# Four tiles with one rest phase in the up projection of an mLSTM and GELU kernel

## The chip, the cores and the metric

The kernel runs on one core of one Trainium2 chip, as one launch. The metric is the time on the device in microseconds (us), the median of several executions.

## The reference

Two parts are joined. The first is an mLSTM cell over batch 4, 8 heads, 768 steps and a head dimension of 40. The second is a plain two-layer network over the 3072 tokens of 320 features that the first part yields.

```python
for t in range(S):
    m_new = maximum(f[t] + m, i[t])
    C = exp(f[t] + m - m_new) * C + exp(i[t] - m_new) * outer(v[t], k[t])
    n = exp(f[t] + m - m_new) * n + exp(i[t] - m_new) * k[t]
    y[t] = sigmoid(o[t]) * (C @ q[t]) / maximum(abs(n @ q[t]), 1.0)
x = y as (B*S, H*D) = (3072, 320)
h = x @ w_in                      # (3072, 2048)
g = 0.5 * h * (1 + erf(h / sqrt(2)))
out = g @ w_out                   # (3072, 320)
```

All inputs are float32 but the two weight matrices, which the kernel converts from 64-bit floats as their bits lie in memory.

## The kernel before

**Stages.** The sequence is cut into six chunks of 128 steps. A chunk of all four batches is 512 tokens (TG). For each chunk the cell part makes x (its transpose, xT, in SBUF), the up step makes g = gelu(x w_in), and the down step makes g w_out. The cell work of chunk c+1 is dealt out between the products of the down step of chunk c. The first chunk and the cell part of the second are played from the string FRONT, in which conversions of the weights, loads, cell steps and up and down steps of chunk 0 are interleaved by hand. The later chunks are played from the string DOWN. So the instruction order on each engine is the written order: the pools are under manual_schedule, and each engine works in order. Semaphores between engines are set from what each instruction reads and writes.

**Letters of FRONT.** O and L load v and o, and q and k; P fetches a piece of weights; K and J are the two halves of a conversion (conv_one: three VectorE and two ScalarE instructions, conv_two: two VectorE instructions); Z adds parts of w_in; E, N, D and Q make the gate sums and decays. m, w, g, t, s, c, v, y, x are the cell steps of chunk 0 (mask, weights, gate, turn, scores, carry, values, finish, turn_y) for a batch, in capitals those of chunk 1. A and U are up steps of chunk 0, F a row of its down step. I n asks for n products into a bank that nobody reads, at the next place that calls unread; a later I before that place replaces it. They keep TensorE from idling.

**The up step of chunks 1 to 5 (summed_up, L589).** x and w_in are cut into blocks of two halves each: w_in by features 0 to 127 and 128 to 255 (x = 0, 1) and by hidden halves (e), x by the same features and by token halves (h). For these 256 features the product of 2 x 2 blocks is done with seven products instead of eight, from sums made ahead: in_sums of w_in (in_sum), x_sums of x (sum_x). The remaining 64 features are added directly, as the rest phase: their products use 64 rows, one hidden half on the upper and one on the lower half of the array (halves, w_rest). f0 counts pairs of hidden tiles, and there are four of them. For each, c11, p6, p5, c22, c12, c21 each take a bank of PSUM (128 x 512 float32) in turn from four kinds of banks, two of each, by bank() (L596). A product (L604) is two matmuls in the code and four matmul instructions in the trace.

The seven products make the four blocks so: c11's first product is copied to g (ScalarE, L611); p6 is added to it (VectorE, L614); p5 is added to that (L617); c22 is added to p6's sum (L620). c12, c21 and the second product of c11 follow; then come the 16 rest instructions (L629). After that ScalarE takes the gelu of c11 (L634), and for c22, c12 and c21 VectorE adds the partial sums (L636) and ScalarE takes the gelu in place (L637).

**Sums of g (hidden_sums, L520).** The down step also uses seven products, from sums s1 and s2 of blocks of g and a block of differences. They are made by three VectorE instructions (L525 to L527) for two tiles each, right after the rest phase of the following pair has been issued. In chunk 1 the sums of w_out for the down step (weight_sum, L507) are made around the up step: the first before it, the second after it, the others within DOWN.

**The down step (down_steps, L661).** Its product (L674) has 16 instructions; the first two (p1) read only g as it stands, the next two (p6) read s2 and, on the other side, the second sum of w_out.

Of the kernel before, what the change touches and what calls it, by code (L numbers as in the profile page):

```python
# [9 lines left out]
F32 = mybir.dt.float32  # L10
BF16 = mybir.dt.bfloat16
U32 = mybir.dt.uint32
AF = mybir.ActivationFunctionType
OP = mybir.AluOpType

P = 128
# [6 lines left out]


FRONT = """
    O0 L0 P0 I3 g0 L2 P1 E I2 t0 N w0 L1 K P2 D w1 Q O2 s0 P3 w2 t1 O1 c0 J v0 K t2 s1 w3 L3 g1 v1 I3 O3 J y0 c1 K
    B5 y1 s2 x0 O4 t3 L4 J x1 K B4 L5 g3 s3 I7 v2 g2 c2 c3 y2 G0 v3 x2 K J A L6 y3 M1 J x3 M0 K H K O7 O5 J T0 J W0
    O6 A S0 K W1 M2 J C0 T1 U U K K Z V0 J T2 L7 A M3 W2 J G1 S1 C1 Z W3 A K K G2 S2 Y0 C2 Z J J K V1 T3 G3 K U U Y1
    S3 Z C3 J V2 K F F F J Z K J J K K J Z K J F F J V3 K X0 K F J Z F J F F F K J K Y2 K J X1 K F F F J K J F J F Z
    X2 B8 B9 Y3 X3 F"""  # L30
DOWN = """
    M0 Z M1 T0 W0 F F T1 W1 Z G3 Z F S0 Z S1 C0 M2 Z C1 G1 G0 M3 V0 Y0 Z V1 W2 Z F F T2 W3 F T3 F G2 Z Y1 S2 S3 C2
    V2 C3 Y2 V3 F F Y3 X0 F F X1 X2 F F X3 F"""
# [3 lines left out]
def kernel(  # L37
# [16 lines left out]
    nc = tc.nc  # L54

    B, H, S, D = q.shape
# [11 lines left out]
    NX = 2  # L68
# [12 lines left out]
    ps_tr = ctx.enter_context(tc.tile_pool(name="ps_tr", bufs=2, space=bass.MemoryType.PSUM))  # L81
    ps_h = ctx.enter_context(tc.tile_pool(name="ps_h", bufs=2, space=bass.MemoryType.PSUM))
    ps_mm = ctx.enter_context(tc.tile_pool(name="ps_mm", bufs=2, space=bass.MemoryType.PSUM))
# [9 lines left out]
    w_rest = const.tile([P, DFF // 2], F32, name="w_rest")  # L93
# [4 lines left out]
    xT = const.tile([P, NX + 1, TG], F32, name="xT")  # L98
# [60 lines left out]
    a = gates.tile([BH, NCH, L], F32, name="a")  # L159
# [114 lines left out]
    def conv_one(i):  # L274

        if i < len(pieces):
            n = bits[i].shape[1]
            lo, hi = bits[i][:, :, 0], bits[i][:, :, 1]
            s = sig[i] = raw.tile([P, WP], F32, name="sig", tag="sig")[:, 0:n]
            p = pow2[i] = raw.tile([P, WP], F32, name="pow", tag="pow")[:, 0:n]  # L280
            su, pu = s.bitcast(U32), p.bitcast(U32)

            nc.vector.tensor_scalar(out=pu, in0=hi, scalar1=20, scalar2=0x7FF,
                                    op0=OP.logical_shift_right, op1=OP.bitwise_and)
            nc.scalar.activation(out=p, in_=pu, func=AF.Relu, scale=-I23, bias=e_hi)
            nc.scalar.activation(out=pu, in_=p, func=AF.Relu, scale=-1.0, bias=e_lo)

            nc.vector.tensor_scalar(out=su, in0=hi, scalar1=0xFFFFF, scalar2=0x100000,
                                    op0=OP.bitwise_and, op1=OP.bitwise_or)
            nc.vector.scalar_tensor_tensor(out=s, in0=lo, scalar=2.0 ** -32, in1=su, op0=OP.mult, op1=OP.add)  # L290
# [15 lines left out]
    halves = (slice(0, R), slice(R, P))  # L306
# [171 lines left out]
    HF, HT, HD = NF // 2, TG // 2, DM // 2  # L478
# [41 lines left out]
    def hidden_sums(g, f0, f1):  # L520

        (a11, a21), (_, a22) = [[g.t[:, HF * e + f0:HF * e + f1, HT * h:HT * (h + 1)] for h in range(2)]
                                for e in range(2)]
        s1, s2 = [t[f0 // (HF // 2)][:, f0 % (HF // 2):f0 % (HF // 2) + f1 - f0, :] for t in (g.s1, g.s2)]
        nc.vector.tensor_tensor(out=s1, in0=a21, in1=a22, op=OP.add)  # L525
        nc.vector.tensor_tensor(out=s2, in0=s1, in1=a11, op=OP.subtract)
        nc.vector.tensor_tensor(out=a21, in0=a11, in1=a21, op=OP.subtract)  # L527
# [24 lines left out]
    def first_up_steps(h):  # L552

        def step(k):
            ups.append((len(ups) + len(tags_next) % 2, (2 * k, 2 * k + 2, HT * h, HT * h + HT)))
            if len(ups) == 2:
                first_up()

        return [lambda k=k: step(k) for k in range(HF // 2)]
# [20 lines left out]
    def x_blocks():  # L580
        return [[xT[:, x, HT * h:HT * (h + 1)] for h in range(2)] for x in range(NX)]
# [7 lines left out]
    def summed_up(g):  # L589
        (a11, s3), (a12, a22) = [[w_in[:, x, e, :] for e in range(2)] for x in range(NX)]  # L590
        s1, s2, s4 = in_sums
        (b11, t3), (b21, b22) = x_blocks()
        t1, t2, t4 = x_sums
        banks = [0]

        def bank():  # L596
            pool, tag = ((ps_tr, "tr"), (ps_h, "h"), (ps_mm, "a"), (ps_mm, "b"))[banks[0] % 4]
            banks[0] += 1
            return pool.tile([P, 2, HT], F32, name="pu", tag=tag)

        def product(to, lhs, rhs, f0, first, last):

            for j in range(2):
                nc.tensor.matmul(to[:, j, :], lhs[:, (f0 + j) * P:(f0 + j + 1) * P], rhs, start=(first and j == 0),  # L604
                                 stop=(last and j == 1), skip_group_check=True)

        for f0 in range(0, HF, 2):
            blk = [[g.t[:, HF * e + f0:HF * e + f0 + 2, HT * h:HT * (h + 1)] for h in range(2)] for e in range(2)]
            c11 = bank()
            product(c11, a11, b11, f0, True, False)  # L610
            nc.scalar.copy(out=blk[1][1], in_=c11)  # L611
            p6 = bank()
            product(p6, s2, t2, f0, True, True)
            nc.vector.tensor_tensor(out=blk[0][0], in0=p6, in1=blk[1][1], op=OP.add)  # L614
            p5 = bank()
            product(p5, s1, t1, f0, True, True)
            nc.vector.tensor_tensor(out=blk[0][1], in0=p5, in1=blk[0][0], op=OP.add)  # L617
            c22 = bank()
            product(c22, s3, t3, f0, True, False)
            nc.vector.tensor_tensor(out=blk[1][0], in0=c22, in1=blk[0][0], op=OP.add)  # L620
            c12 = bank()
            product(c12, s4, b22, f0, True, False)
            c21 = bank()
            product(c21, a22, t4, f0, True, False)
            product(c11, a12, b21, f0, False, False)
            for h, pair in ((0, (c11, c21)), (1, (c12, c22))):
                for j in range(2):
                    for e in range(2):
                        nc.tensor.matmul(pair[e][:, j, :], w_rest[halves[e], (f0 + j) * P:(f0 + j + 1) * P],  # L629
                                         xT[halves[e], NX, HT * h:HT * (h + 1)], start=False, stop=(j == 1),  # L630
                                         skip_group_check=True)
            if f0 > 0:
                hidden_sums(g, f0 - 2, f0)
            nc.scalar.activation(out=blk[0][0], in_=c11, func=AF.Gelu)  # L634
            for e, h, x, y in ((1, 1, c22, blk[0][1]), (0, 1, c12, blk[0][1]), (1, 0, c21, blk[1][0])):
                nc.vector.tensor_tensor(out=blk[e][h], in0=x, in1=y, op=OP.add)  # L636
                nc.scalar.activation(out=blk[e][h], in_=blk[e][h], func=AF.Gelu)  # L637
        hidden_sums(g, HF - 2, HF)

    def send(c, b, o_sb):  # L640
        nc.sync.dma_start(out=out[b * S + c * L:b * S + (c + 1) * L, :], in_=o_sb)
# [1 line left out]
    def first_down_steps(g):  # L643
        po = []

        def row(f):

            if f == 0:
                po.extend(ps_mm.tile([P, DM], F32, name="po", tag="ab"[b // 2]) for b in range(B))
            for b in range(B):  # L650
                nc.tensor.matmul(po[b], g.t[:, f, b * L:(b + 1) * L], w_out[:, f, :], start=(f == 0),  # L651
                                 stop=(f == NF - 1))
                if f == NF - 1:
                    if b % 2 == 0:
                        o_sb = outp.tile([P, 2, DM], F32, name="o_sb", tag="o_sb")
                    nc.scalar.copy(out=o_sb[:, b % 2, :], in_=po[b])
                    send(0, b, o_sb[:, b % 2, :])

        return [lambda f=f: row(f) for f in range(NF)]
# [71 lines left out]
    def in_turn(steps):  # L731
        todo = list(steps)
        return lambda: todo.pop(0)() if todo else None

    def cell_steps(c, letters):
# [8 lines left out]
                 A=in_turn(first_up_steps(0)), U=in_turn(first_up_steps(1)), F=in_turn(first_down_steps(first_g)),  # L744
                 K=in_turn(lambda i=i: conv_one(i) for i in n_pieces), H=sums_begin,
                 J=in_turn(lambda i=i: conv_two(i) for i in n_pieces), Z=in_turn(lambda i=i: in_sum(i) for i in range(8)))
    steps |= cell_steps(0, "mwgtscvyx") | cell_steps(1, "MWGTSCVYX")
    play(FRONT, steps)
    for c in range(1, NCH):
        g, later = Hidden(True), []  # L750
# [42 lines left out]
```

## Time and profile before

523.43 us, the median of three (523.29 to 523.52). The profiled execution spans 521.7 us.

| what | value |
|---|---|
| TensorE busy | 503.5 us, 4460 matmul instructions |
| VectorE busy | 341.2 us, 711 instructions |
| ScalarE busy | 254.7 us, 522 instructions |
| products of the up step, L604 | 560 instructions in five stages |
| rest phase, L629 | 320 instructions, 40.0 us busy |
| first product of the up step of chunk 1 | 135.6 us after the start |
| last rest instruction | about 487.8 us after the start |

[...]how long a phase lasts is read from where instructions start, not from their mean duration. In the timeline and the groups, the first numbers are start and length in us, then engine, line and operation, with what it writes and reads, the shapes and the count; a bracket gives the idle time of the engine ahead of it and what ended it. "issue" in a bracket means that no other engine was waited for. PE is TensorE, PEld its weight loads, DVE VectorE, ACT ScalarE, POOL GpSimd.

### The profile page before, as it was taken

The page shows a single profiled execution, that of the slowest core. Times are in us where ns is not written, and L with a number is a line of the kernel's source. Part 1 is how long each engine was busy: PE and PEld are TensorE (multiplying, and loading weights), DVE is VectorE, ACT ScalarE, POOL GpSimd, SP SyncE. Part 2 cuts the span into 40 slices and gives each one's busy share as a digit, 9 for nine tenths or more (in the row PEclk, how much of TensorE's full clock was granted, in tenths as well). Part 3 has the DMA queues.
Part 4 walks back from the last instruction along what each step waited for, and adds up shares of the span by engine and source line. Part 5 has one row for each costly group of instructions (what it writes and reads, how often), then busy time and mean ns, then how long its engine had stood idle before and what let it go on. Part 6 is the DMA issues. An engine that isn't in the chain of part 4 may idle for free.

```text
span 521.7 us, 10943 instructions
## 1 busy us (share of the span) xinstructions
PE 503.5 (97%) x4460; PEld 448.0 (86%) x4460; DVE 341.2 (65%) x711; ACT 254.7 (49%) x522; POOL 60.1 (12%) x98
## 2 busy tenths in 40 slices
PE   4779999999999999999999999999999999999997
PEld 3568888877788999988999988999988999988997
DVE  7579788999577887367578357478356657256621
ACT  5786999654243970232980134782134583134200
POOL 3001010000200134000054000053000021000000
PEclk9699999999999999999999999999999999999999
DMA  8898950369710234900134900124930020000001
GB/s 172 165 205 176 234 126 20 81 173 188 142 53 1 81 105 61 172 0 2 41 108 70 175 25 1 35 88 80 158 58 1 0 83 2 26 25 2 1 0 52
DMA packets 111442, 41.62 MB, mean 80 GB/s; under 512 B 101184, under 2 KB 104416, under 8 KB 111392
## 3 DMA queue, kind: packets, MB, share of 16 engines
q1 hardware_dynamic: 111392, 40.92, 38.5%
q8 instruction: 35, 0.57, 0.5%
q14 instruction: 15, 0.12, 0.1%
HBM read 36.90 MB, written 4.01 MB: 78 GB/s over the span
## 4 chain that ended last, share of the span: by engine, by line
PE 93%; DVE 3%; ACT 2%; issue 1%; DMA 0%; SPq 0%; DVEq 0%; ACTq 0%
PE po L674 30%; PE pu L604 24%; PE pu L629 7%; PE po L651 7%; PE pu L538 5%; PE ps L395 4%; PE ph L444 4%; PE pt L373 4%; PE pf L419 2%; PE pf L414 2%; PE px L470 1%; PE pu L544 1%; DVE M L194 1%; ACT W L359 0%; DMA i_sb<-in_i_gate_dram 0%
## 5 line engine op out<-in xcount | busy, mean ns | idle before, releaser
L674 PE MATMUL po<-w_out,g 128*128 128x160 f32 x640 | 91.5, 299 | 0.0
L674 PEld LDWEIGHTS po<-w_out,g 128*128 128x128 f32 x640 | 88.0, 190 | 0.3 <-issue 0.3
L604 PE MATMUL pu<-xT,w_in 128*128 128x256 f32 x240 | 63.2, 386 | 0.0
L636 DVE TENSOR_TENSOR g<-pu,g 128x512 f32<-128x512 f32 x60 | 39.6, 688 | 34.4 <-PE pu L629 33.8
L604 PEld LDWEIGHTS pu<-xT,w_in 128*128 128x128 f32 x240 | 44.1, 190 | 10.3 <-issue 5.0
L398 DVE TENSOR_TENSOR W<-ps,W 128x512 f32<-128x512 f32 x48 | 30.2, 684 | 32.5 <-ACT W L359 20.6
L359 ACT ACTIVATE W<-Mb,aT 128x128 f32<-128x128 f32 x160 | 49.0, 392 | 0.1
L471 ACT COPY xT<-px 128x384 f32<-128x384 f32 x24 | 11.0, 480 | 77.3 <-PE px L470 77.3
L634 ACT ACTIVATE g<-pu 128x512 f32<-128x512 f32 x20 | 11.9, 597 | 74.1 <-PE pu L629 74.1
L637 ACT ACTIVATE g<-g 128x512 f32<-128x512 f32 x60 | 37.2, 630 | 22.1 <-DVE g L636 20.2
L674 PE MATMUL po<-w_sums,sums 128*128 128x160 f32 x320 | 47.3, 302 | 0.0
L674 PEld LDWEIGHTS po<-w_sums,sums 128*128 128x128 f32 x320 | 44.0, 190 | 0.4
L334 POOL TENSOR_SCALAR_AFFINE_SELECT Mb<-Mb 128x1024 f32<-128x1024 f32 x20 | 22.1, 1113 | 188.8 <-DMA Mb<-M_d 188.4
L629 PE MATMUL pu<-xT,w_rest 64*128 64x256 f32 x320 | 40.0, 389 | 0.0
L687 DVE TENSOR_TENSOR o_sb<-po,o_sb 128x320 f32<-128x320 f32 (+1 forms) x27 | 12.5, 463 | 41.5 <-PE po L674 36.2
L604 PE MATMUL pu<-x_sums,in_sums 128*128 128x256 f32 x160 | 37.8, 379 | 0.0
L629 PEld LDWEIGHTS pu<-xT,w_rest 64*128 64x128 f32 x320 | 29.3, 186 | 9.3 <-issue 6.6
L651 PE MATMUL po<-w_out,g 128*128 128x320 f32 x128 | 35.2, 433 | 0.0
L604 PEld LDWEIGHTS pu<-x_sums,in_sums 128*128 128x128 f32 x160 | 30.4, 190 | 4.1
L651 PEld LDWEIGHTS po<-w_out,g 128*128 128x128 f32 x128 | 24.0, 190 | 9.5
L432 POOL TENSOR_TENSOR state<-state,dec 64x164 f32<-64x164 f32 x24 | 11.2, 465 | 162.2 <-PE pf L419 158.4
L538 PE MATMUL pu<-xT,w_in 128*128 128x256 f32 x128 | 28.8, 381 | 0.5 <-DVE W L398 0.5
(138 smaller groups left out, 869.3 us busy)
## 6 DMA issues: line engine op xcount, KB each, us to landing
Mb<-M_d SPq DMA_DIRECT2D x20, 512.0 KB, 3.9
bits<-in_moe_w_in_dram SPq DMA_DIRECT2D x20, 256.0 KB, 4.2
bits<-in_moe_w_out_dram SPq DMA_DIRECT2D x16, 320.0 KB, 3.4
vb<-in_v_dram SPq DMA_DIRECT2D x24, 160.0 KB, 4.8
ob<-in_o_gate_dram SPq DMA_DIRECT2D x24, 160.0 KB, 4.0
qb<-in_q_dram SPq DMA_DIRECT2D x24, 160.0 KB, 4.2
kb<-in_k_dram SPq DMA_DIRECT2D x24, 160.0 KB, 4.6
out_dram<-o_sb SPq DMA_DIRECT2D x24, 160.0 KB, 3.1
```

Of the source, the lines that this page charges most:

```text
L334: nc.gpsimd.affine_select(out=t, in_=t, compare_op=OP.is_ge, fill=1.0e30, base=0, pattern=[[0, H], [1, L]], channel_multiplier=-1)
L359: nc.scalar.activation(out=W[n][:, h, :], in_=src, func=AF.Exp, scale=-1.0, bias=aT[:, self.c, r:r + 1])
L373: nc.tensor.transpose(pt[:, p, :], src[n % NLD][:, 2 * p:2 * p + 2, :].rearrange("p h d -> p (h d)"), ident)
L395: nc.tensor.matmul(ps[hip][:, p, :], kT[r, p, :], qT[r, p, :], start=True, stop=True)
L398: nc.vector.tensor_tensor(out=w, in0=ps[hip], in1=w, op=OP.mult)
L538: nc.tensor.matmul(banks[-1][e][:, i - i0, :], w_in[:, x, e, i * P:(i + 1) * P], xT[:, x, t0:t1], start=(x == 0 and i == i0), stop=False, ...
L604: nc.tensor.matmul(to[:, j, :], lhs[:, (f0 + j) * P:(f0 + j + 1) * P], rhs, start=(first and j == 0), stop=(last and j == 1), skip_group_c ...
L629: nc.tensor.matmul(pair[e][:, j, :], w_rest[halves[e], (f0 + j) * P:(f0 + j + 1) * P], xT[halves[e], NX, HT * h:HT * (h + 1)], start=False ...
L636: nc.vector.tensor_tensor(out=blk[e][h], in0=x, in1=y, op=OP.add)
L637: nc.scalar.activation(out=blk[e][h], in_=blk[e][h], func=AF.Gelu)
L651: nc.tensor.matmul(po[b], g.t[:, f, b * L:(b + 1) * L], w_out[:, f, :], start=(f == 0), stop=(f == NF - 1))
L674: nc.tensor.matmul(bank[at][:, i, :], lhs(j, t), rhs(j), start=(first and i == 0 and j == 0), stop=(i == n - 1 and j == HF - 1), skip_grou ...
```

## The change

Two pairs of hidden tiles (four tiles) now go together. All eight banks are taken, four for each pair: c11, c12, c21 and c22. The products p6 and p5 no longer have banks of their own; they go to those of c12 and c21, and once VectorE has read them the later products of these blocks start in the same banks. The second product of c11 moves ahead of c12 and c21. When both sets of seven products are issued, one rest phase follows for both, first for the blocks with h = 0, then for h = 1. The gelus and adds come after it: both c11, then both c21, then c22 and c12 of each pair. The sums of g of the first four tiles are made two tiles at a time within the second group, those of the last four in one go after it. The aim is that TensorE changes between the full-height and the 64-row shape half as often.

The string FRONT is replaced by another order of the same steps, with six more I steps. It has the same loads, conversions, cell, up and down steps; among others w0 stands ahead of t0, N and the decays D ahead of the first conversion K, y0 ahead of w3, W0 and W1 earlier, and G3 and V3 later.

```diff
--- before.py
+++ after.py
@@ -23,11 +23,11 @@
 
 
 FRONT = """
-    O0 L0 P0 I3 g0 L2 P1 E I2 t0 N w0 L1 K P2 D w1 Q O2 s0 P3 w2 t1 O1 c0 J v0 K t2 s1 w3 L3 g1 v1 I3 O3 J y0 c1 K
-    B5 y1 s2 x0 O4 t3 L4 J x1 K B4 L5 g3 s3 I7 v2 g2 c2 c3 y2 G0 v3 x2 K J A L6 y3 M1 J x3 M0 K H K O7 O5 J T0 J W0
-    O6 A S0 K W1 M2 J C0 T1 U U K K Z V0 J T2 L7 A M3 W2 J G1 S1 C1 Z W3 A K K G2 S2 Y0 C2 Z J J K V1 T3 G3 K U U Y1
-    S3 Z C3 J V2 K F F F J Z K J J K K J Z K J F F J V3 K X0 K F J Z F J F F F K J K Y2 K J X1 K F F F J K J F J F Z
-    X2 B8 B9 Y3 X3 F"""
+    O0 L0 I1 I1 g0 E L1 P0 O2 P1 w0 t0 N D K w1 L2 P2 Q P3 s0 O1 t1 w2 L3 c0 J K v0 K s1 y0 w3 t2 I3 g1 v1 O3 I2 I3
+    I5 J c1 B5 I2 K y1 I4 I2 s2 x0 O4 L4 t3 J x1 B4 s3 v2 I7 g3 L5 g2 c2 c3 y2 v3 x2 O5 L6 K J G0 A y3 x3 J H M0 M1
+    K K J T0 W0 O6 M2 O7 A J W1 S0 C0 K J T1 L7 U U K Z K V0 T2 A M3 J J G1 S1 K W2 W3 K C1 Z A S2 Z V1 G2 J Y0 J K
+    C2 Z T3 J K Y1 U U J S3 Z V2 C3 K J K K J J F K F F F Z J K J X0 K K J F F F Z J F K G3 Y2 F J K V3 J K F K X1 J
+    J F F F F K Z X2 B8 J F Y3 X3 B9 F"""
 DOWN = """
     M0 Z M1 T0 W0 F F T1 W1 Z G3 Z F S0 Z S1 C0 M2 Z C1 G1 G0 M3 V0 Y0 Z V1 W2 Z F F T2 W3 F T3 F G2 Z Y1 S2 S3 C2
     V2 C3 Y2 V3 F F Y3 X0 F F X1 X2 F F X3 F"""
@@ -591,51 +591,56 @@
         s1, s2, s4 = in_sums
         (b11, t3), (b21, b22) = x_blocks()
         t1, t2, t4 = x_sums
-        banks = [0]
-
-        def bank():
-            pool, tag = ((ps_tr, "tr"), (ps_h, "h"), (ps_mm, "a"), (ps_mm, "b"))[banks[0] % 4]
-            banks[0] += 1
-            return pool.tile([P, 2, HT], F32, name="pu", tag=tag)
-
         def product(to, lhs, rhs, f0, first, last):
 
             for j in range(2):
                 nc.tensor.matmul(to[:, j, :], lhs[:, (f0 + j) * P:(f0 + j + 1) * P], rhs, start=(first and j == 0),
                                  stop=(last and j == 1), skip_group_check=True)
 
-        for f0 in range(0, HF, 2):
+        def products(f0, to_sum):
+
             blk = [[g.t[:, HF * e + f0:HF * e + f0 + 2, HT * h:HT * (h + 1)] for h in range(2)] for e in range(2)]
-            c11 = bank()
+            c11, c12, c21, c22 = [pool.tile([P, 2, HT], F32, name="pu", tag=tag)
+                                  for pool, tag in ((ps_tr, "tr"), (ps_h, "h"), (ps_mm, "a"), (ps_mm, "b"))]
             product(c11, a11, b11, f0, True, False)
             nc.scalar.copy(out=blk[1][1], in_=c11)
-            p6 = bank()
-            product(p6, s2, t2, f0, True, True)
-            nc.vector.tensor_tensor(out=blk[0][0], in0=p6, in1=blk[1][1], op=OP.add)
-            p5 = bank()
-            product(p5, s1, t1, f0, True, True)
-            nc.vector.tensor_tensor(out=blk[0][1], in0=p5, in1=blk[0][0], op=OP.add)
-            c22 = bank()
+            product(c12, s2, t2, f0, True, True)
+            nc.vector.tensor_tensor(out=blk[0][0], in0=c12, in1=blk[1][1], op=OP.add)
+            product(c21, s1, t1, f0, True, True)
+            nc.vector.tensor_tensor(out=blk[0][1], in0=c21, in1=blk[0][0], op=OP.add)
             product(c22, s3, t3, f0, True, False)
             nc.vector.tensor_tensor(out=blk[1][0], in0=c22, in1=blk[0][0], op=OP.add)
-            c12 = bank()
+            if to_sum > 0:
+                hidden_sums(g, f0 - 4, f0 - 2)
+            product(c11, a12, b21, f0, False, False)
             product(c12, s4, b22, f0, True, False)
-            c21 = bank()
             product(c21, a22, t4, f0, True, False)
-            product(c11, a12, b21, f0, False, False)
-            for h, pair in ((0, (c11, c21)), (1, (c12, c22))):
-                for j in range(2):
-                    for e in range(2):
-                        nc.tensor.matmul(pair[e][:, j, :], w_rest[halves[e], (f0 + j) * P:(f0 + j + 1) * P],
-                                         xT[halves[e], NX, HT * h:HT * (h + 1)], start=False, stop=(j == 1),
-                                         skip_group_check=True)
-            if f0 > 0:
-                hidden_sums(g, f0 - 2, f0)
-            nc.scalar.activation(out=blk[0][0], in_=c11, func=AF.Gelu)
-            for e, h, x, y in ((1, 1, c22, blk[0][1]), (0, 1, c12, blk[0][1]), (1, 0, c21, blk[1][0])):
-                nc.vector.tensor_tensor(out=blk[e][h], in0=x, in1=y, op=OP.add)
-                nc.scalar.activation(out=blk[e][h], in_=blk[e][h], func=AF.Gelu)
-        hidden_sums(g, HF - 2, HF)
+            return f0, blk, ((c11, c21), (c12, c22))
+
+        def rest(f0, pair, h):
+            for j in range(2):
+                for e in range(2):
+                    nc.tensor.matmul(pair[e][:, j, :], w_rest[halves[e], (f0 + j) * P:(f0 + j + 1) * P],
+                                     xT[halves[e], NX, HT * h:HT * (h + 1)], start=False, stop=(j == 1),
+                                     skip_group_check=True)
+
+        for group in ((0, 2), (4, 6)):
+
+            sets = [products(f, group[0]) for f in group]
+            for h in range(2):
+                for f, _, pairs in sets:
+                    rest(f, pairs[h], h)
+            for _, blk, ((c11, _), _) in sets:
+                nc.scalar.activation(out=blk[0][0], in_=c11, func=AF.Gelu)
+            add_to = lambda blk, e, h, x, y: (
+                nc.vector.tensor_tensor(out=blk[e][h], in0=x, in1=y, op=OP.add),
+                nc.scalar.activation(out=blk[e][h], in_=blk[e][h], func=AF.Gelu))
+            for _, blk, ((_, c21), _) in sets:
+                add_to(blk, 1, 0, c21, blk[1][0])
+            for _, blk, (_, (c12, c22)) in sets:
+                add_to(blk, 1, 1, c22, blk[0][1])
+                add_to(blk, 0, 1, c12, blk[0][1])
+        hidden_sums(g, HF - 4, HF)
 
     def send(c, b, o_sb):
         nc.sync.dma_start(out=out[b * S + c * L:b * S + (c + 1) * L, :], in_=o_sb)
```

## The prediction

> **What bounds the kernel now.** I read the busy table first, then the chain of waits, then the timeline of one up stage, then the start of the run by windows.
>
> ```profile
> PE 503.5 (97%) x4460; PEld 448.0 (86%) x4460; DVE 341.2 (65%) x711; ACT 254.7 (49%) x522; POOL 60.1 (12%) x98
> ...
> PE 93%; DVE 3%; ACT 2%; issue 1%; DMA 0%; SPq 0%; DVEq 0%; ACTq 0%
> ```
>
> TensorE is busy 97% and 93% of the chain is TensorE. Only what takes time off TensorE, or makes it wait, moves the end. The chain in order of time shows a later up stage (chunk 3):
>
> ```profile
> 296.48 6.04 PE pu L604 x28
> 302.52 1.93 PE pu L629 x16
> 304.45 6.24 PE pu L604 x28
> 310.69 1.93 PE pu L629 x16
> 312.62 6.24 PE pu L604 x28
> ...
> 327.03 1.93 PE pu L629 x16
> ```
>
> Four blocks, each of seven products (28 instructions, since a product is four) and a rest phase of 16, without a gap on TensorE. All five stages look so. The products of a block take 6.04 us where they follow other full-height work and 6.24 us where they follow a rest phase, whose operands have 64 rows. The timeline shows both changes of shape:
>
> ```profile
> 296.32 1.03 PE L604 MATMUL pu<-xT,w_in 128*128 128x256 f32 x4
> ...
> 302.45 1.60 PEld L629 LDWEIGHTS pu<-xT,w_rest 64*128 64x128 f32 x16 [0.33 <-issue]
> 302.45 2.00 PE L629 MATMUL pu<-xT,w_rest 64*128 64x256 f32 x16
> 303.62 0.60 ACT L634 ACTIVATE g<-pu 128x512 f32<-128x512 f32 x1 [1.59 <-PE pu L629]
> 304.38 0.73 PEld L604 LDWEIGHTS pu<-xT,w_in 128*128 128x128 f32 x4 [0.33 <-issue]
> 304.38 1.13 PE L604 MATMUL pu<-xT,w_in 128*128 128x256 f32 x4
> 304.50 2.01 DVE L636 TENSOR_TENSOR g<-pu,g 128x512 f32<-128x512 f32 x3 [3.83 <-PE pu L629]
> 305.22 1.95 ACT L637 ACTIVATE g<-g 128x512 f32<-128x512 f32 x3 [1.01 <-DVE g L636]
> 307.08 0.57 ACT L611 COPY g<-pu 128x512 f32<-128x512 f32 x1
> 307.69 0.69 DVE L614 TENSOR_TENSOR g<-pu,g 128x512 f32<-128x512 f32 x1 [1.17 <-ACT g L611]
> ```
>
> At 302.45 and 304.38 the weight load stands idle 0.33 us for "issue": no engine is waited for. The pitch of a product's instructions is 6.04/28 = 0.216 us. Rest instructions run two at a time on the two halves, so 16 should last 8 x 0.216 = 1.73 us, but they take 1.93. So one change into the 64-row shape costs 0.20, one back 6.24 - 6.04 = 0.20: **0.40 us for a round trip**, four times a stage.
>
> **What the skill says.** "TensorEngine Tiling (Array Packing)", Key Properties: changing the tiling mode drains the TensorE. The trace agrees and gives the price the page lacks, 0.20 us each way. "TensorE: Matmul & The Clock Gate", Architectural detail: ScalarE and VectorE are strict FIFO, while TensorE only pulls weight loads ahead. The trace agrees: the copy L611 at 307.08 had its product ready long before and started when the three gelus ahead of it were through. The same page, What's actually happening: an idle array has half its clock and gets the whole one after some 3.4 us of work. That bears on the new order of the front; the clock of 0.61 from 13 to 26 us in the windows below agrees.
>
> **Part 1, one rest phase for four tiles.** Two round trips instead of four in each of five stages: 5 x 2 x 0.397 (0.40 unrounded, from single starts) = **-3.97 us** of TensorE time. Instruction counts don't change.
>
> **Part 2, banks and order of products.** The sixth and fifth products now sit in the banks of the blocks c12 and c21, and a second product starts there once VectorE has read the first. New waits: c11's second product for the copy L611; c12's for the add L614; c21's for L617. Each set of seven begins at t, with 0.863 us (4 x 0.216) a product. First group: c11 ends at t+1.03, copy 1.06 to 1.64 (297.38 in the trace is 1.06 after 296.32), L614 from 2.0 to 2.69, L617 to 3.48. The products that need these start at t+3.45, 4.32 and 5.18. Nothing waits, with 0.8 us or more to spare.
>
> The second group is the tight one: ScalarE must do eight gelus before it copies c11 again. Count from R, the start of the first rest phase (16 pairs: 3.45 + 0.20 = 3.66 us). c11 of the two sets is whole at R+1.13 and 2.00. Gelus of c11: 1.17 and 2.03 to 2.63. VectorE's six adds at 0.67 each (2.01/3): c21 at 1.19 and 2.05, then the four of the second half from 2.92 to 5.59. ScalarE's other six gelus at 0.66 follow without gap from 2.63 to 6.56, always behind their add. Copy of the new c11: R+6.47 to 7.04. Its second product is due at 3.66 + 0.10 + 4 x 0.863 = R+7.21. **Slack 0.17 us.** The bank of the new c12 is free at 4.27 and wanted at 4.62. L614 ends at 7.77 (c12 due at 8.07), L617 at 8.56 (due at 8.94). The sums of g of two tiles (three of 0.69) end at R+11.1; the next set's L614 can't start before 11.7. So I count nothing here; upper bound, if each of these hand-overs is 0.1 us slower than shown, is some 0.5 to 0.8 us a stage, 4 us in all.
>
> Banks at the stage's start: the last sum of the down step (L687) is read by 297.0, and c22, the first to need a "b" bank, comes at 298.9. Costs nothing. The table load for gelu (1.28 us) comes after the second copy and before the first gelu, 4 us apart, as idle ScalarE time.
>
> **Part 3, after the stage.** Let E be the end of rest. ScalarE ends its gelus at E+2.90 (before: E+2.81), so the copies and W behind them on its queue move by 0.1 to 0.2 us; they have that slack, since scores come at E+8.4. The sums of g now wait for the very last gelu and take four tiles in one go (1.22 us each, the row of L700 with the same 128x1024): s1 to E+4.17, s2 to 5.4, the third to 6.6. Before, s2 was ready at E+3.65. The product that reads s2 begins at E+6.15 (E+4.45 in the last chunk); its first four tiles come from the other half of s2, long ready, and the fifth is wanted 1.1 us later, at 5.5 in the last chunk. Just enough: 0 to 0.2. But in chunk 1 the eight subtractions of the second weight sum (L507, 1.97 us) are queued behind these sums: their first lands at E+6.85 instead of before 6.15, so TensorE waits some 0.8 us; if it must wait for all eight, 2.4. I take **+0.8** once.
>
> **Part 4, the order of the front.**
>
> ```profile
> 0.00:13.00 13.00, 5.35 (x30) 4.24 (x30) 10.17 (x31) 7.16 (x13) 4.55 (x26) 1.00 0.88 173
> 13.00:26.00 13.00, 9.85 (x74) 7.72 (x74) 7.39 (x20) 9.12 (x30) 0.00 (x0) 0.61 0.89 164
> 26.00:39.00 13.00, 10.06 (x160) 8.50 (x158) 10.24 (x25) 11.25 (x26) 1.09 (x1) 1.00 0.95 205
> 39.00:52.00 13.00, 12.22 (x165) 10.63 (x164) 12.58 (x29) 8.20 (x17) 1.49 (x1) 1.00 0.83 176
> 52.00:60.20 8.20, 7.74 (x83) 6.50 (x81) 5.88 (x12) 8.09 (x17) 0.00 (x0) 1.00 1.28 212
> ...
> 98.50:133.50 35.00, 35.00 (x167) 25.07 (x166) 32.31 (x87) 15.12 (x29) 0.00 (x0) 1.00 0.77 146
> ```
>
> (The columns are length, then busy time of TensorE, weight load, VectorE, ScalarE, GpSimd, clock, DMA.) TensorE idles 15 us in the first 60 and nowhere later, so only there can the order help or harm. For: w0 comes before t0 and N, so its exponentials fill ScalarE's 2.6 us of waiting near 11 to 13.8; decay copies (D) come ahead of the first conversion, which held them from 14.3 to 15.6. Together the first scores, at 20.35 now, may start 1 to 1.3 us sooner. W0's exponentials before the second A may also remove the 0.46 us wait at 60.2. Against: 18 instead of 12 units of unread matmuls (2 instructions each, 0.11 us, so 6 x 0.22 = 1.3 us), five of them at c1; a third conversion ahead of v1; and VectorE is busy 32.31 of 35 us in the last window, where ScalarE (97% busy from 60.2 to 98.5) and VectorE must also keep up with a TensorE that comes earlier. Bounds: -3 and +3; I take **-0.6**.
>
> **Sum**: -3.97 + 0.8 - 0.6 = -3.8; 523.43 - 3.8 = **519.7 us**.
>
> **Rivals.**
> 1. The copy behind eight gelus comes late and c11, c12, c21 wait in turn, 0.8 us in each of five stages: -3.97 + 0.8 + 4.0 - 0.6 = +0.2, **523.6 us**. For it: a slack of 0.17, and strict FIFO. Against: every link is priced by a row of the same operation. Chance 0.14.
> 2. The front loses: the fills cost their 1.3 us, the moved conversions 1.7 more (+3), chunk 1 waits for all eight subtractions (+2.4), stages lose 0.3 each (+1.5): 523.4 - 4.0 + 6.9 = **526.3 us**, slower. For it: the busy windows above. Against: equal counts of conversions (five) before the first up step. Chance 0.13.
> 3. The front gains more, 3 us of its 15 idle, with no wait in chunk 1: 523.4 - 4.0 - 3.0 = **516.5 us**. Against: the last window of VectorE has 2.7 us to give. Chance 0.13.
>
> Forecast 0.60. The range, 517.0 to 523.8, takes in rival 1 and cuts off rival 2 and half of rival 3, 0.2 in all. Faster by over 0.2%: the forecast, rival 3 and a third of rival 1, 0.78; rest of rival 1 partly within, 0.07; slower, rival 2 and a little of 1, 0.15.
>
> **What would show it.** Rest phases in the chain: ten of 32 instructions at about 3.66 us instead of twenty of 1.93. Products: 56 in some 12.1 us, twice a stage. A stage (first product to first transpose) about 31.8 us instead of 32.57. L611's third copy ending 0.1 to 0.2 us before c11's second product. In chunk 1 a wait of TensorE for L507 near 0.8. The end of the front, now 135.6, at about 135. It is wrong if TensorE shows waits for L611, L614 or L617 in the second group, or if the first product of chunk 1 starts later than 136.5.

## The result and the profile after

The changed kernel takes 518.52 us (517.16 to 518.68) against 523.47: a ratio of 0.990, 95% interval 0.9883 to 0.9917, so 4.95 us less. 519.7 was forecast. The profiled executions span 516.9 and 521.7 us.

The busy table and the chain's shares, after:

```profile
PE 501.4 (97%) x4472; PEld 451.0 (87%) x4472; DVE 340.4 (66%) x696; ACT 255.0 (49%) x523; POOL 61.3 (12%) x98
...
PE 90%; ACT 4%; DVE 4%; issue 1%; DMA 0%; SPq 0%; DVEq 0%; ACTq 0%
```

Twelve more matmul instructions (the fills), yet less busy time. TensorE is still what sets the end. The chain in order of time (start, length, line, count) for the stage of chunk 2:

```profile
214.42 12.09 PE pu L597 x56
226.50 3.65 PE pu L623 x32
230.16 12.28 PE pu L597 x56
242.44 3.65 PE pu L623 x32
246.10 1.02 PE pt L373 x8
```

Two rest phases of 32 instructions instead of four of 16, and no other engine between. Where the time went is read from the starts of single instructions in the two traces; durations can't be summed, as a product's instruction lasts 0.38 us and the next one starts 0.216 us after it.

| stretch | before, us | after, us | difference | forecast |
|---|---|---|---|---|
| start to the first product of chunk 1 | 135.56 | 134.12 | -1.43 | -0.6 |
| each of five up stages | 32.57 | 31.77 | -0.80, in all -3.98 | -3.97 |
| end of rest to next stage, chunk 1 | 47.81 | 48.36 | +0.55 | +0.8 |
| the same, chunks 2 and 3 | 47.81 | 47.81 | 0.00 | 0 to 0.2 |
| the same, chunk 4 | 45.94 | 45.94 | 0.00 | 0 to 0.2 |
| end of the last rest to the last product | 30.40 | 30.40 | 0.00 | 0 to 0.2 |
| sum | | | -4.86 | -3.8 |

The spans differ by the same 4.87 us. The tight place of the forecast, in the timeline of chunk 1's second group (each line: start, length, engine, line, operation):

```profile
146.30 3.72 PE L623 MATMUL pu<-xT,w_rest 64*128 64x256 f32 x32
148.82 3.82 ACT L637 ACTIVATE g<-g 128x512 f32<-128x512 f32 x6
149.24 2.74 DVE L636 TENSOR_TENSOR g<-pu,g 128x512 f32<-128x512 f32 x4 [0.17 <-PE pu L623]
149.96 1.13 PE L597 MATMUL pu<-xT,w_in 128*128 128x256 f32 x4
152.55 0.57 ACT L606 COPY g<-pu 128x512 f32<-128x512 f32 x1
152.65 1.89 PE L597 MATMUL pu<-xT,w_in 128*128 128x256 f32 x8
```

The copy L606 does stand behind the gelus (they run to 152.64), but it ends at 153.12. The eight instructions from 152.65 are c22 and then the second product of c11, whose first starts at 152.65 + 4 x 0.216 = 153.51. The slack is 0.39 us, not 0.17: the row of six gelus began 2.52 us after the start of the rest phase where 2.63 was reckoned, and each took 0.64 us instead of 0.66. Nothing waits. The one new wait is in the down step of chunk 1. Before, its product that reads the second sum (L674) started right behind the transposes (L373):

```profile
172.30 1.97 DVE L507 TENSOR_TENSOR w_sums<-w_out,w_sums 128x160 f32<-128x160 f32 x8
...
173.85 0.60 PE L373 MATMUL pt<-ident,qb 128*128 128x128 f32 x4
...
174.28 2.34 PE L674 MATMUL po<-w_sums,sums 128*128 128x160 f32 x16
```

After:

```profile
169.85 1.22 DVE L526 TENSOR_TENSOR sums<-sums,g 128x1024 f32<-128x1024 f32 x1
170.99 1.22 DVE L527 TENSOR_TENSOR g<-g 128x1024 f32<-128x1024 f32 x1
...
171.61 0.60 PE L373 MATMUL pt<-ident,qb 128*128 128x128 f32 x4
172.12 1.97 DVE L507 TENSOR_TENSOR w_sums<-w_out,w_sums 128x160 f32<-128x160 f32 x8
172.50 2.44 PE L679 MATMUL po<-w_sums,sums 128*128 128x160 f32 x16 [0.28 <-DVE w_sums L507]
```

The product starts just after the first of the eight subtractions, not after all of them. From the last transpose (171.94) to it there are 0.56 us, where 0.11 is the pitch of such instructions: 0.45 us of waiting. The remaining 0.10 us of the 0.55 comes right behind it: the product's second instruction starts 0.24 us after the first, where 0.136 is the pitch.

### The profile page after: what moved, and what is told of

Its sections match the earlier page's. It is cut to its first block, busy times and chain, and to the rows that moved or that the text cites. A ratio compares the mean times of both kernels' runs of the same rounds, so it can differ in the third digit from the quotient of the medians.

```text
span 516.9 us, 10957 instructions
## 1 busy us (share of the span) xinstructions
PE 501.4 (97%) x4472; PEld 451.0 (87%) x4472; DVE 340.4 (66%) x696; ACT 255.0 (49%) x523; POOL 61.3 (12%) x98
## 4 chain that ended last, share of the span: by engine, by line
PE 90%; ACT 4%; DVE 4%; issue 1%; DMA 0%; SPq 0%; DVEq 0%; ACTq 0%
PE po L679 29%; PE pu L597 24%; PE pu L623 7%; PE po L656 7%; PE pu L538 5%; PE ps L395 4%; PE ph L444 4%; PE pt L373 3%; PE pf L419 2%; PE pf L414 2%; PE pu L544 1%; PE px L470 1%; ACT W L359 1%; ACT pow L285 1%; DVE M L194 1%
## 5 line engine op out<-in xcount | busy, mean ns | idle before, releaser
L597 PE MATMUL pu<-xT,w_in 128*128 128x256 f32 x240 | 58.8, 381 | 0.0
L636 DVE TENSOR_TENSOR g<-pu,g 128x512 f32<-128x512 f32 x60 | 40.6, 690 | 24.2 <-PE pu L623 22.8
L334 POOL TENSOR_SCALAR_AFFINE_SELECT Mb<-Mb 128x1024 f32<-128x1024 f32 x20 | 23.3, 1175 | 186.0 <-DMA Mb<-M_d 126.3
L398 DVE TENSOR_TENSOR W<-ps,W 128x512 f32<-128x512 f32 x48 | 30.3, 684 | 22.9 <-PE ps L395 20.2
L606 ACT COPY g<-pu 128x512 f32<-128x512 f32 x20 | 11.6, 582 | 58.2 <-PE pu L597 58.2
L623 PE MATMUL pu<-xT,w_rest 64*128 64x256 f32 x320 | 37.2, 382 | 0.0
L637 ACT ACTIVATE g<-g 128x512 f32<-128x512 f32 x60 | 36.1, 627 | 1.9
L608 DVE TENSOR_TENSOR g<-pu,g 128x512 f32<-128x512 f32 x20 | 13.8, 692 | 34.6 <-PE pu L597 28.7
```

The costliest lines, as they stand in the source:

```text
L334: nc.gpsimd.affine_select(out=t, in_=t, compare_op=OP.is_ge, fill=1.0e30, base=0, pattern=[[0, H], [1, L]], channel_multiplier=-1)
L398: nc.vector.tensor_tensor(out=w, in0=ps[hip], in1=w, op=OP.mult)
```

## The experiments

**The two parts alone.** up_only is the changed kernel with the old FRONT; front_only the old one with the new FRONT.

```diff
 FRONT = """
-    O0 L0 I1 I1 g0 E L1 P0 O2 P1 w0 t0 N D K w1 ...     (new)
+    O0 L0 P0 I3 g0 L2 P1 E I2 t0 N w0 L1 K P2 D w1 ...  (old: up_only; the reverse in the kernel before: front_only)
```

> The new up step with the old order of the front. Theory (the changes of shape cost 0.40 us a round trip, and the front's order adds to it on its own): five stages of 31.77 us instead of 32.57, the wait of chunk 1 for the weight sums of some 0.5 us stays, the first product of chunk 1 starts at 135.6 as before; time about 519.9 to 520.0. Rival (the new front gains only together with the new up step, or the up step carries all): about 518.5.

Measured: 520.37 us, ratio 0.9936 (0.9923 to 0.9948), 3.42 us below the kernel before (523.79). The stages last 31.77 us, the first product of chunk 1 comes at 135.56, and chunk 1's down step takes 48.36. So the up step is worth -3.98 + 0.55 = -3.43 in the trace, and the medians agree.

> The old up step with the new order of the front. Theory: the front ends 1.4 us sooner and nothing else changes; time about 522.0, the first product of chunk 1 at 134.1. Rival: no gain without the new up step, 523.4.

Measured: 521.77 us, ratio 0.9962 (0.9949 to 0.9976), 2.0 us less. Stages 32.57, first product at 134.16: the order of the front gains without the new up step. In the traces the two parts add up: 3.43 and 1.40 us, of 4.86.

**More changes of shape.** rest_each keeps banks, products and sums, and takes a rest phase after each set of seven.

```diff
-            sets = [products(f, group[0]) for f in group]
-            for h in range(2):
-                for f, _, pairs in sets:
-                    rest(f, pairs[h], h)
+            sets = []
+            for f in group:
+                sets.append(products(f, group[0]))
+                for h in range(2):
+                    rest(f, sets[-1][2][h], h)
```

> The changed kernel, but with a rest phase after each set of seven products, so four a stage again; banks, order of products, sums of g and gelus stay as changed. Theory of the shape changes: ten round trips of 0.397 come back, stages of 32.57 us, time about 522.5. Rival (the gain comes from the banks or from the larger sums of g): stays at about 518.5.

Measured: 526.23 us, ratio 1.0048 (1.0035 to 1.0061): the sign of the theory, and more than it said. Four of the stages last 33.12 us, not 32.57. Its timeline shows why:

```profile
230.28 2.00 PE L623 MATMUL pu<-xT,w_rest 64*128 64x256 f32 x16
231.49 3.34 DVE L637 TENSOR_TENSOR g<-pu,g 128x512 f32<-128x512 f32 x5 [2.40 <-PE pu L623]
...
232.21 1.13 PE L597 MATMUL pu<-xT,w_in 128*128 128x256 f32 x4
233.62 1.59 PEld L597 LDWEIGHTS pu<-x_sums,in_sums 128*128 128x128 f32 x8 [0.68 <-PE pu L597]
233.65 1.97 PE L597 MATMUL pu<-x_sums,in_sums 128*128 128x256 f32 x8 [0.31 <-DVE g L637]
```

The next group's p6 wants the bank of c12 at 232.21 + 0.10 + 4 x 0.216 = 233.17. But the adds that empty it are written behind the add of c21 of the second set, which waits for the second rest phase; p6 starts at 233.65. In the changed kernel the longer joint rest phase covers these adds. In the last stage, which took 33.83, the first down product waits for the same adds as well, and the down step of chunk 1 takes 48.98 us instead of 48.36.

To part the two effects, rest_each_own issues each set's gelus and adds together:

```diff
-            for _, blk, ((c11, _), _) in sets:
-                nc.scalar.activation(out=blk[0][0], in_=c11, func=AF.Gelu)
...
-            for _, blk, ((_, c21), _) in sets:
+            for _, blk, ((c11, c21), (c12, c22)) in sets:
+                nc.scalar.activation(out=blk[0][0], in_=c11, func=AF.Gelu)
                 add_to(blk, 1, 0, c21, blk[1][0])
-            for _, blk, (_, (c12, c22)) in sets:
                 add_to(blk, 1, 1, c22, blk[0][1])
                 add_to(blk, 0, 1, c12, blk[0][1])
```

> As rest_each (a rest phase after each set, four a stage), but each set's gelus and adds are issued together, so that the first set's blocks are read while the second set's products run, and no bank comes free late. Theory (in rest_each 0.80 us of the 1.34 a stage were two round trips of shape, and 0.55 a wait for the bank of c12 behind the adds): stages of exactly 32.57 us, no wait of TensorE for the adds, 3.97 us above the changed kernel, some 522.4. Rival (the bank wait belongs to having p6 in the bank of c12, whatever the order): stages of 33.1 us and 525 to 526.

Measured: 524.78 us, ratio 1.0028 (1.0016 to 1.0040), against 518.26 for the changed kernel on the same chip. All five stages last 32.57 us: two round trips cost 2 x 0.398 us, whatever the banks. The total missed by 2.4 us, since another wait came after the stage: 0.90 us more from the end of rest to the next stage for chunks 2 to 4 (48.71 instead of 47.81, for chunk 4 46.84 instead of 45.94) and 0.35 more in chunk 1. This trace's front ended 1.0 us sooner, which hides a part of it. The stage of chunk 2 ends so:

```profile
244.46 0.68 DVE L527 TENSOR_TENSOR g<-g 128x512 f32<-128x512 f32 x1
...
245.06 3.93 DVE L635 TENSOR_TENSOR g<-pu,g 128x512 f32<-128x512 f32 x6
...
247.64 0.58 ACT L638 ACTIVATE g<-pu 128x512 f32<-128x512 f32 x1
...
248.27 0.42 PEld L373 LDWEIGHTS pt<-ident,qb 128*128 128x128 f32 x4 [0.92 <-ACT g L638]
248.28 0.66 PE L373 MATMUL pt<-ident,qb 128*128 128x128 f32 x4 [0.68 <-ACT g L638]
```

In this second group the edit does not do what was expected of it: VectorE's six adds, those of the first set too, are written behind the sums of g, and start only with the second rest phase, at 245.06. The gelu of the second c11 stands behind the first set's three gelus on ScalarE, which wait for those adds; and the transposes want its bank. The changed kernel's order, both c11 first, avoids it.

**The slack of the copy.** c11_early moves c11's second product ahead of c22's.

```diff
+            product(c11, a12, b21, f0, False, False)
             product(c22, s3, t3, f0, True, False)
...
-            product(c11, a12, b21, f0, False, False)
```

> The changed kernel with the second product of c11 one product earlier, ahead of c22's. Theory (ScalarE's copy of c11 behind eight gelus is what comes next: in the second group it ends at R+6.82, R the start of the rest phase, and the product would be due at R+6.35): TensorE waits some 0.5 us for the copy once a stage, 2.5 us in all, about 521.0. Rival (the copy has much more room than that): 518.5.

Measured: 521.33 us, ratio 0.9956 (0.9944 to 0.9969). Stages of 32.39 us: 0.62 more in each of five, 3.1 in all. The waits of TensorE name the copy, five times:

```profile
PE pu L597 <- ACT g L606: 1.8, 5, 0.4
```

So the eight gelus ahead of the copy are what comes next on the path: the change leaves 0.39 us, and one product (0.863 us) less uses it up with some 0.5 us over. The 0.62 us are this wait and 0.10 us behind it: after the wait the second instruction starts 0.32 us after the first, where 0.216 is the pitch. Rival 1 was near, but was not there.

**The wait in chunk 1.** ws_early issues the second weight sum ahead of the last sums of g.

```diff
-    def summed_up(g):
+    def summed_up(g, ahead):
...
+        for step in ahead:
+            step()
         hidden_sums(g, HF - 4, HF)
...
-        summed_up(g)
-        if c == 1:
-            for step in weight_sum(2):
-                step()
+        summed_up(g, weight_sum(2) if c == 1 else [])
```

> The changed kernel, with the second weight sum of chunk 1 issued ahead of the last sums of g instead of behind them. Theory (TensorE waits in chunk 1 because these subtractions are queued behind the sums of four tiles): that wait of 0.45 us goes, time about 518.0. Rival (then the last sums of g are late by the 1.97 us of the subtractions and TensorE waits for them instead): the wait stays or grows, 518.5 to 519.5.

> ws_early once more, beside the changed kernel on the same chip. The wait of chunk 1 is gone (0.55 us); the rest of its lead came from an array that had its whole clock 2.4 us sooner in that profile. So 0.5 us below the changed kernel, some 517.8; if the other lead were its own, 1.0 below or more.

Measured: 517.48 us, ratio 0.9882 (0.9868 to 0.9896); again 517.75, ratio 0.9882 (0.9863 to 0.9900), beside 518.13 for the changed kernel on that chip. In both traces the down step of chunk 1 is back at 47.81 us:

```profile
166.79 1.96 DVE L507 TENSOR_TENSOR w_sums<-w_out,w_sums 128x160 f32<-128x160 f32 x8
168.67 1.22 DVE L525 TENSOR_TENSOR sums<-g 128x1024 f32<-128x1024 f32 x1
...
171.03 2.34 PE L681 MATMUL po<-w_sums,sums 128*128 128x160 f32 x16
```

The subtractions run in part while VectorE would have waited for the last gelus, which end at 167.54. The sums start 1.1 us later than in the changed kernel, counted from the end of rest (3.79 us after it instead of 2.69), and the product can bear it: it starts 6.15 us after the end of rest, as in the kernel before, without a wait. The 0.55 us is shown by the traces; the medians (0.38 apart beside the changed kernel) are within their intervals. It has the lowest medians of the versions tried.

**The front.** no_fills leaves out all unread matmuls, which compute nothing that is used.

```diff
-    O0 L0 I1 I1 g0 E L1 ...
+    O0 L0 g0 E L1 ...            (and so on for every I)
```

> The changed kernel without any of the unread matmuls of the front (36 instructions left out, whose results nobody reads). Theory A (they cost time on TensorE's path, as the prediction counted for the added six): the front ends 0.5 to 2 us sooner, 516.5 to 518. Theory B (they lie in waits and keep TensorE's clock whole): no gain; the front ends as before or, with a longer stretch at half clock, 1 to 3 us later, 518.5 to 521.5.

Measured: 518.70 us, ratio 0.9907 (0.9894 to 0.9921), beside 518.26: no difference that the intervals part. The first product of chunk 1 comes at 134.44 (134.08 with the fills), and TensorE idles 10.3 instead of 7.4 us between its first instruction and this product. The windows (columns as in the prediction; the clock is the third from the right) show half clock coming back:

```profile
32.00:36.00 4.00, 4.00 (x31) 3.77 (x29) 3.05 (x9) 3.90 (x8) 0.00 (x0) 0.57 0.90 265
36.00:43.00 7.00, 5.01 (x118) 4.34 (x115) 6.39 (x16) 3.20 (x9) 0.00 (x0) 0.98 0.87 189
43.00:46.00 3.00, 3.00 (x11) 2.55 (x10) 2.86 (x8) 2.08 (x4) 0.93 (x1) 0.50 1.20 211
```

So Theory A falls: leaving the fills out gains nothing at the end of the front. The first up step (L538) does start sooner, at 43.64 us instead of 44.51. But this array had its whole clock sooner too, at 22.23 us instead of 24.20; ws_early, with all its fills and the whole clock at 21.81, starts that step at 43.53. So the lead there is not shown to come from the missing fills. The next up step then starts 7.10 us later instead of 5.87, as the first one lies in the half clock from 42.70 to 46.12 us.

front_head and front_tail take one half of the old order each, divided at s0 (in both, P3 is placed so that each piece is fetched once).

```diff
 FRONT = """
     O0 L0 I1 I1 g0 E L1 P0 O2 P1 w0 t0 N D K w1 L2 P2 Q P3 s0     (new up to here)
-    O1 t1 w2 L3 c0 J K v0 K s1 y0 ...                             (new)
+    w2 t1 O1 c0 J v0 K t2 s1 w3 ...                               (old: front_head; front_tail is the opposite)
```

> The changed kernel, with the new order of the front only up to s0 and the old order (with its fills) behind it. Theory (the front's gain is the one the prediction named: w0 ahead of N, D ahead of the first conversion, so the first scores at 18.95 instead of 20.35 us): most of the 1.4 us stays, the first product of chunk 1 near 134.2, time about 518.5. Rival (the gain is made behind s0, by the moved conversions and y0, and the lead at s0 is lost in the old tail's waits): the first product near 135.5, about 519.9.

> The counterpart: the old order up to s0, the new order behind it. Theory (the gain is made ahead of s0): the first product of chunk 1 near 135.4, about 519.8. Rival (the gain is made behind s0): near 134.2, about 518.5.

> The changed kernel as it is, to compare the other three with on the same chip: about 518.3, the first product of chunk 1 near 134.1.

Measured: front_head 518.48 us (ratio 0.9899, 0.9879 to 0.9918), front_tail 519.59 (0.9918, 0.9901 to 0.9935), the changed kernel beside them 518.13. The first product of chunk 1 comes at 133.35, 135.11 and 133.59. The larger part of the gain is made ahead of s0; the new tail alone gives 0.45 us in the trace (135.56 to 135.11). The clock's moment is a rival here, as front_head's array had its whole clock at 21.78 us, sooner than most. But front_tail and the changed kernel's second trace had it at the same time (24.23 and 24.20) and differ by 1.03 us at the first product (135.11 and 134.08), and the medians put front_head beside the changed kernel. How much of the lead the old tail keeps, front_head's trace alone does not say. The changed kernel ran once more beside other variants:

> The changed kernel as it is, beside the variants on the same chip, to compare them with. About 518.5; stages of 31.77 us, the wait for the weight sums in chunk 1 of 0.55 us, the first product of chunk 1 between 133 and 134.5.

Measured: 518.26 us, ratio 0.9900 (0.9886 to 0.9913), as before, with the first product at 134.08.

## Why the prediction was right

**Part 1** held to 0.01 us: -3.98 against -3.97, and rest_each_own gives the price back exactly when the changes of shape come back. That a drain of TensorE lies behind it is what the Trainium skill says ("TensorEngine Tiling (Array Packing)", Key Properties); the runs show its cost only.

**Part 2** held: no wait in the stage. The slack of 0.17 us was 0.39, since the gelus began a little sooner and were a little shorter. c11_early shows that this slack was a real limit.

**Part 3** had the mechanism right and its size half as large again as measured: +0.8 forecast, +0.55 measured. The term that was off is the end of the gelus, the same row as in Part 2. With E the end of rest, it was reckoned at E+2.90 and came at E+2.65 (164.76 + 3.79 - 165.90). The three sums behind it, of 1.22 us as reckoned, therefore ended at E+6.3 (172.21 - 165.90) instead of E+6.6. The bound "all eight subtractions" (2.4) was not reached.

**Part 4** is the step whose size was wrong: -0.6 forecast, -1.43 measured. Both moves that it named are in the traces: W0's exponentials start at 9.32 instead of 14.90, and the decay copies at 14.26 instead of 15.64. Before:

```profile
14.90 2.09 ACT L359 ACTIVATE W<-pm,aT 128x128 f32<-128x128 f32 x8
...
15.64 0.22 DVE L185 COPY ewT<-pg 128x64 f32<-128x64 f32 x1
```

After:

```profile
9.32 2.18 ACT L359 ACTIVATE W<-pm,aT 128x128 f32<-128x128 f32 x8 [0.21 <-PE pm L356]
...
14.26 0.20 DVE L185 COPY ewT<-pg 128x64 f32<-128x64 f32 x1
...
18.95 2.08 PE L395 MATMUL ps<-qT,kT 64*128 64x128 f32 x16
```

The chain of waits tells which of the two set the first scores (L395). Before, an instruction of the conversion (L290) stands in it between the gate sums and L214, the product that reads a decay copy:

```profile
13.72 0.60 DVE gg L205
15.04 0.69 DVE sig L290
16.02 0.64 PE pd L214 x2
...
20.42 2.01 PE ps L395 x16
```

After, it is gone:

```profile
13.72 0.60 DVE gg L205
14.61 0.64 PE pd L214 x2
...
19.02 2.01 PE ps L395 x16
```

That is 1.41 us at L214, 1.40 at the first scores and 1.43 at the end of the front. W0's exponentials are on neither chain up to there, so a gain from them is not shown. Two other terms failed, with opposite signs. The deduction for the fills (1.3 us) did not come: no_fills shows no cost of all 18 units, though no run leaves out the six new ones alone. And the hope for the 0.46 us wait at 60.2 did not come true either: ahead of the same product, now at 58.67, TensorE still waits 0.5 us for L398. The fear that VectorE or ScalarE would not keep up failed too: in the last 35 us, 1.43 us sooner (97.07 to 132.07), VectorE is busy 31.18 us instead of 32.31, and TensorE has no gap there.

Rivals 1 and 2 didn't come, nor did rival 3's full 3 us with no wait in chunk 1; the front gave half of those 3 us and chunk 1 took part of it back. Of the 1.06 us by which the sum of the stretches differs from the forecast, 0.83 are Part 4 and 0.25 Part 3.

## What to carry to other kernels

Where a loop on the bounding engine switches between two forms of the same operation, price one round trip from the gap in starts and batch the forms; the saving is that price times the trips taken out, provided that the batch also leaves time for what empties the banks. The order of emptying is part of such a change: the same products with another order of adds and gelus lost 0.55 us in the stage or 0.9 us behind it. When sums are batched on an in-order engine, look at what is queued behind them; independent work belongs ahead of the wait.

## What the runs showed of the hardware that was not expected

After a stretch at half clock, the array got its whole clock at another moment in each run, and the end of the front moved along with it, though not strictly. For the changed kernel it came at 24.49, 24.20 and 23.44 us, with the first product of chunk 1 at 134.12, 134.08 and 133.59; in ws_early at 21.81 with 133.11; but in c11_early, whose front is the same, at 23.44 with 134.00. In the thirteen traces that record the moment, it came 3.2 to 5.5 us after the start of the first scores, where the prediction names some 3.4 us of work. Single instructions show it too: the transposes L373 start 0.213 us apart ahead of it and 0.109 behind it. Where a trace has no clock record, the windows print 1.00 all the same, as for up_only from 20 to 24 us, where the transposes are still 0.213 apart. In nine traces with this front its end lies between 133.09 and 134.16 us. So a gain below 1 us must be read from fixed stretches of the trace behind the front, which repeat to 0.004 us.

A wait of TensorE cost some 0.1 us more than its gap: the second instruction behind it came 0.32 instead of 0.216 us after the first in c11_early, 0.29 in rest_each, and 0.24 instead of 0.136 in chunk 1. The same 0.32 stands behind each change back from the 64-row shape, as half of its 0.20 us.

And leaving out work of TensorE (no_fills) did not shorten the front (134.44 us against 134.08), although TensorE bounds the kernel.
